# Attention and a two-layer MLP on one core: the Strassen product of the first layer from chunk 3 on instead of chunk 4

## The chip, the cores and the metric

The kernel runs on one core of a Trainium2 chip. A core has a matrix engine (TensorE, PE in the profile), a vector engine (VectorE, DVE), an engine for activations (ScalarE, ACT), a general one (GpSimd, POOL), a queue engine (SyncE, SP) and 16 DMA engines. They work side by side and wait for each other through semaphores. The metric is the device time of one launch in microseconds, as the median of several runs; less is better.

## The reference

Two parts follow each other. The first is attention with a sliding window of 128 positions and 4 sink positions, for 4 batches, 8 heads, 768 positions and 64 columns a head. The second takes the result as rows x of 512 columns:

```python
xn = (x - mu) / sqrt(var + 1e-6) * g_ln            # over the 512 columns
out = x + maximum(xn @ w_ch1, 0.0) @ w_ch2         # 512 -> 2048 -> 512
```

All inputs and the output are float32; the kernel works in bfloat16 with float32 sums.

## The kernel before

**Tiles and chunks.** The 3072 rows are 24 tiles of 128 rows. Two tiles are a chunk, so there are 12 chunks, three for each batch (R = 0, 1, 2 in the code). They are counted from 0 here, as in the code: the fourth chunk is chunk 3.

**What a chunk goes through.** Its q, k and v are loaded by DMAs on GpSimd's queue (lines 585 and 683). From chunk 4 on, q and k are turned by DMA transposes on SP's queue (line 685, which issues through the helper of line 565), once the scores of the chunk before are done. TensorE makes the scores in two halves (line 788), ScalarE the exponentials (line 802), VectorE multiplies by the mask (line 814). TensorE multiplies by v, one tile at a time (lines 833 and 838). VectorE then makes the rows: reciprocal, x, mean and variance (lines 852 to 860); GpSimd makes the root (lines 866 and 867); VectorE normalises (`xc`, line 869); from chunk 2 on SP turns the rows by DMA transposes (`xnt`, line 879, through the same helper). Then comes the MLP: the first layer into `hq`, the second into the output.

**Two forms of the first layer.** The plain form has eight groups `ph` of eight matmuls with 256 columns each (line 1011) and a relu for each (line 1021). From chunk `half` on, the first four of them are made by a Strassen product (Winograd's variant), `halves`, line 911: GpSimd makes four differences of `xnt` (line 922), TensorE seven products m1 to m7 of eight matmuls with 128 columns each (line 942), ScalarE copies three of them (`tz`, line 953), VectorE makes three totals (line 964), and ScalarE applies the relu to these (line 967) and to the fourth block (line 985). The products m5, m6, m7 and m3 use sums of the weights. These sums are made once, by four VectorE instructions (`weight_sums`, lines 897 to 909), into two buffers of the ring `hq`, which has eight; every chunk uses two.

**The second layer.** From chunk 2 on (`wino=2`) it is a Strassen product as well (`wino`, line 1058): sums of `hq` on VectorE (line 1076), seven products p1 to p7 on TensorE (line 1093), and additions on VectorE (lines 1107 and 1114).

**What sets the order.** No engine chooses anything at run time. The class `Plan` (line 65) simulates the kernel in the build: every operation has the engines that may take it, estimated times, the operations and buffers that it needs, and a due time (`prio`). In each step the planner takes the engine whose next operation can start first, and of those that can start within 0.25 units of that (0.2 on TensorE, 0 on SP) the one with the earliest due time. TensorE's operations with a due time of 40 or more go strictly by due time. The operations are issued in the order of their planned starts, so each engine's order is fixed. The planner's clock is an estimate; it runs some units behind the measured time.

**Due times that matter here.** With T = 16c + 8 for chunk c, the products of `halves` are due at T + `pos`, the four `ph` groups left at T + `pos4`, and the products of the second layer at T + 8.5 + 8/7 i. The attention of chunk c has its steps at

```python
def at(c, step):
    return 16.0 * c - 8.0 + (PAR["h"] if c > PAR["half"] else PAR)[step]
```

so `half` also divides the chunks into those whose attention goes by the numbers of `h` and those that go by the outer ones (`tr=-8.0, sc=-5.3, sc1=-2.0, av=2.0, avi=1.0`). In `h`, `tr` is for the transposes of q and k (the loads are due 14 before), `sc` and `sc1` for the two halves of the scores, `av` for the values, `avi` for the distance of the second tile, and `xo` for VectorE's row chain against `av`. Two more things hang on `c > half`: in chunks with R > 0 the mask of the first head pair (`mkp=(0,)`) is made by GpSimd in two instructions (line 809, due at `mko` behind the scores), not by VectorE. And from chunk `half` on, the planner reckons with a later landing of the transposed rows (`xlag`, line 880).

The other numbers: `wsum` is the due time of the first weight sum and the earliest planned start (the others 3 apart); `tlead` puts GpSimd's differences ahead, `tzp` the copies, `cpr` the totals; `sp` and `sq` place the sums of `hq` for the second layer, `kp` its additions.

Of the kernel before, what the change touches and what calls it, by code (L numbers as in the profile page):

```python
# [220 lines left out]
def fix(occ, extra=0.09):  # L221
# [17 lines left out]

PAR = dict(split=(3, 4, 5, 6, 7), gsum=-8.0, guard=183.0, strict=40.0, win=0.4, tr=-8.0, sc=-5.3, sc1=-2.0, av=2.0, trx=9.0, by_dma=4, x_by_dma=2, g_on_w=2, av2=20.0, avi=1.0, behind=5, gtt=9.0, ramp=0.3, vs0=2.6, vpb=12.0,  # L240
           w1p=(0.15, 1.7, 2.05, 2.8), pm=2, w2p=(4.5, 4.51, 4.52, 4.53), by_tile=2, wino=2, vp=(0.0, 0.1, 2.0, 2.1, 4.2, 4.3), ld1=0.05,
           h=dict(av=0.85, avi=-0.0, sc=-7.68, sc1=-2.94, tr=-24.25, trx=9.0, xo=-13.3), mkp=(0,), mko=-3.93, vsp=1, soon=0, lb=0, xlag=2.1, llag=2.4, mix=(1.0, 0.5), tzp=20.19, kp=-0.95, half=4, wsum=58.0, flip=1, te=("POOL",), tlead=58.56, rd=0, cpr=15.35, sp=(10.27, 4.87), sq=(-1.16, -17.0, 5.05, 17.16), pos=(-1.36, 0.58, 4.21, 6.8, 1.47, 1.55, 4.55), pos4=(4.77, 3.73, 4.73, 5.69))


def general(tc, nc, slots, pairs, ones, ident_f, ident, w1, w2, mhalf, g_s, g_r, q, k, v, out, scale):
# [1018 lines left out]
```

## Time and profile before

| | us |
|---|---|
| median of 3 runs | 209.54 |
| lowest and highest run | 208.6, 209.82 |
| the profiled execution's own time | 209.8 |
| its span, first to last instruction | 208.3 |
| PE busy in the span | 200.6 |
| DVE busy | 177.7 |
| ACT busy | 122.3 |
| POOL busy | 117.0 |

The span and the busy times are of one profiled execution. The busy time of TensorE is modelled from pipelined instructions. The mean granted clock of TensorE was 0.998 of full speed. A row of the profile names the line of the kernel, the engine, the operation, and the tiles written and read (`hq<-one`: from a PSUM bank `one` into `hq`). Operations that a helper issues carry the helper's line: all DMA transposes stand under line 565.

### The profile page before, as it was taken

The page shows a single profiled execution, that of the slowest core. Times are in us where ns is not written, and L with a number is a line of the kernel's source. Part 1 is how long each engine was busy: PE and PEld are TensorE (multiplying, and loading weights), DVE is VectorE, ACT ScalarE, POOL GpSimd, SP SyncE. Part 2 cuts the span into 40 slices and gives each one's busy share as a digit, 9 for nine tenths or more (in the row PEclk, how much of TensorE's full clock was granted, in tenths as well). Part 3 has the DMA queues.
Part 4 walks back from the last instruction along what each step waited for, and adds up shares of the span by engine and source line. Part 5 has one row for each costly group of instructions (what it writes and reads, how often), then busy time and mean ns, then how long its engine had stood idle before and what let it go on. Part 6 is the DMA issues. An engine that isn't in the chain of part 4 may idle for free.

```text
span 208.3 us, 6722 instructions
## 1 busy us (share of the span) xinstructions
PE 200.6 (96%) x2736; PEld 168.1 (81%) x2736; DVE 177.7 (85%) x433; ACT 122.3 (59%) x190; POOL 117.0 (56%) x170
## 2 busy tenths in 40 slices
PE   6978999999999999999999999999999999999994
PEld 2657897774698898997898997998988988998993
DVE  6579767999699898898879989989989979997783
ACT  3549379919455646466486586585586486471520
POOL 7965565369129119949639957888638038035000
PEclk9999999999999999999999999999999999999999
DMA  6999999999999999999999999999974511211202
GB/s 120 151 192 191 200 188 206 194 163 133 177 187 135 116 205 89 113 201 90 175 146 116 139 154 123 121 165 128 190 115 81 151 28 28 102 28 25 107 26 84
DMA packets 101245, 27.53 MB, mean 132 GB/s; under 512 B 89556, under 2 KB 99032, under 8 KB 101208
## 3 DMA queue, kind: packets, MB, share of 16 engines
q0 software_dynamic: 67712, 13.37, 77.8%
q1 hardware_dynamic: 33208, 13.41, 36.6%
q8 instruction: 22, 0.36, 0.7%
q10 hardware_dynamic: 288, 0.26, 0.4%
q14 instruction: 15, 0.12, 0.2%
HBM read 27.30 MB, written 6.29 MB: 161 GB/s over the span
## 4 chain that ended last, share of the span: by engine, by line
PE 85%; DMA 9%; POOL 3%; issue 1%; DVE 0%; SPq 0%
PE one L1093 28%; PE one L1011 20%; PE one L942 12%; PE one L1042 7%; DMA w<-in_moe_w_ch_dram 7%; PE one L1004 5%; PE pair L838 5%; PE pair L788 4%; DMA xnt<-xc 2%; PE pair L833 2%; PE one L668 1%; POOL nat L622 1%; POOL vn L585 1%; PE one L792 1%; POOL w L543 1%; POOL n4b L598 1%
## 5 line engine op out<-in xcount | busy, mean ns | idle before, releaser
L802 ACT ACTIVATE pe<-pair 128x1024 bf16<-128x1024 f32 (+1 forms) x40 | 36.3, 966 | 17.0 <-PE pair L788 17.0
L1011 PE MATMUL one<-xnt,w 128*128 128x256 bf16 x384 | 45.5, 273 | 0.0
L1021 ACT ACTIVATE hq<-one 128x512 bf16<-128x512 f32 x58 | 34.1, 594 | 19.4 <-PE one L1011 9.6
L1011 PEld LDWEIGHTS <-w 128*128 128x128 bf16 x384 | 36.6, 98 | 4.1
L1093 PEld LDWEIGHTS <-hs 128*128 128x128 bf16 x320 | 30.6, 98 | 3.9 <-DVE hs L1076 0.2
L866 POOL TENSOR_SCALAR st<-st 128x1 f32<-128x1 f32 x24 | 5.6, 235 | 44.3 <-DVE st L860 30.3
L967 ACT ACTIVATE hq<-hq 128x512 bf16<-128x512 bf16 x24 | 15.1, 628 | 19.7 <-DVE hq L964 19.7
L814 DVE TENSOR_TENSOR pe<-pe,mask 128x1024 bf16<-128x1024 bf16 (+1 forms) x35 | 25.5, 757 | 0.9 <-ACT pe L802 0.8
L1093 PEld LDWEIGHTS <-hq 128*128 128x128 bf16 x240 | 22.3, 98 | 4.1 <-issue 0.3
L585 POOL DMA_DIRECT2D vn<-in_v_dram x24 | 21.9, 920 | 3.2 <-DMA w<-in_moe_w_ch_dram 1.8
L953 ACT COPY tz<-one 128x512 f32<-128x512 f32 x24 | 13.3, 583 | 12.5 <-PE one L942 12.3
L1093 PE MATMUL one<-w,hq 128*128 128x256 bf16 x160 | 19.2, 273 | 0.0
L922 POOL TENSOR_TENSOR xt<-xnt 128x256 bf16<-128x256 bf16 x16 | 13.4, 855 | 8.9 <-DMA xnt<-xc 8.9
L1114 DVE TENSOR_TENSOR ot<-one,tm 128x256 f32<-128x256 f32 x40 | 16.2, 414 | 2.3 <-PE one L1093 1.9
L1107 DVE TENSOR_TENSOR tm<-one,x 128x256 f32<-128x256 f32 x40 | 16.7, 416 | 1.7 <-PE one L1093 1.5
L1076 DVE TENSOR_TENSOR hs<-hq 128x512 bf16<-128x512 bf16 x40 | 15.7, 421 | 2.5 <-ACT hq L1021 1.9
L1004 PE MATMUL one<-xnt,w 128*128 128x128 bf16 x256 | 16.3, 219 | 0.7 <-DVE xnt L891 0.5
L854 DVE TENSOR_TENSOR x<-pair,rec 128x512 bf16<-128x512 f32 x24 | 16.4, 691 | 0.7
L964 DVE TENSOR_TENSOR hq<-one,tz 128x512 bf16<-128x512 f32 x24 | 16.1, 674 | 0.7 <-PE one L942 0.4
L1004 PEld LDWEIGHTS <-w 128*128 128x128 bf16 x256 | 14.7, 98 | 2.0 <-issue 0.5
L683 POOL DMA_DIRECT2D nat<-in_k_dram x16 | 14.9, 930 | 2.5 <-DMA w<-in_moe_w_ch_dram 2.5
L683 POOL DMA_DIRECT2D nat<-in_q_dram x16 | 14.2, 898 | 3.6 <-DMA w<-in_moe_w_ch_dram 3.6
(131 smaller groups left out, 394.3 us busy)
## 6 DMA issues: line engine op xcount, KB each, us to landing
out_dram<-ot SPq DMA_DIRECT2D x17, 256.0 KB
w<-in_moe_w_ch_dram POOLq DMA_DIRECT2D x8, 512.0 KB, 13.1
vn<-in_v_dram POOLq DMA_DIRECT2D x24, 128.0 KB, 7.1
nat<-in_k_dram POOLq DMA_DIRECT2D x17, 128.0 KB, 4.8
nat<-in_q_dram POOLq DMA_DIRECT2D x17, 128.0 KB, 5.1
out_dram<-ot SPq DMA_DIRECT2D x14, 128.0 KB
kq<-nat SPq DMA_TRANSPOSE x32
xnt<-xc SPq DMA_TRANSPOSE x20
```

The source lines that it names most:

```text
L585: loads[b * RB + r, "v"] = P.op(f"vld{t}", {"POOL": (0.87, 0.9)}, prio, lambda e: G.dma_start(bv.t[:, :, 0:64], v[b, :, 128 * r:128 * (r + ...
L683: lambda e, nat=nat, ap=ap: G.dma_start(nat.t, ap), writes=[nat], dma=SW if c < 6 else (*SW[:2], PAR["llag"]), after=behind(c, 0 if soon e ...
L802: P.op(f"ex{c}{hp}", {"ACT": act(2 * n)}, d + 0.1 + 0.05 * j, lambda e, pp=pp, pb=pb: nc.scalar.activation(pb.t[:, :, 0:n], pp.t[:, :, 0:n ...
L814: V.tensor_mul(pb.t[:, :, 0:n], pb.t[:, :, 0:n], mm),
L854: P.op(f"x{t}", {"DVE": dve(512)}, d + xo + 0.11, lambda e: V.tensor_tensor(x.t.rearrange("p (a h c) -> p a h c", a=2, c=64), pv()[:, :, : ...
L942: nc.tensor.matmul(b.t[:, 128 * h:128 * h + 128], lhsT=lt[:, kk, 128 * h:128 * h + 128], rhs=rh[:, kk, :], start=first and h == 0 and kk = ...
L1004: nc.tensor.matmul(ph.t[:, 128 * s:128 * s + 128], lhsT=w1[u // 2][:, j, 128 * s:128 * s + 128], rhs=xnt.t[:, j, 128 * (u % 2):128 * (u % ...
L1011: nc.tensor.matmul(ph.t[:, 256 * s:256 * s + 256], lhsT=w1[ht // 4][:, j, 128 * (ht % 4):128 * (ht % 4 + 1)], rhs=xnt.t[:, j, :], start=j ...
L1021: nc.scalar.activation(hg.t[:, u % 4, :], ph.t, AF.Relu)
L1093: nc.tensor.matmul(at(r), lhsT=get(left, g)[:, v, s, :], rhs=rhs, start=first and n == 0, stop=n == 7, skip_group_check=True)
L1107: return P.op(f"tm{name}_{c}", {"DVE": dve(256, 1.14)}, pr - PAR["kp"], lambda e: V.tensor_tensor(tm[name].t, at(r), xs[i].t[:, sl], op=AL ...
L1114: return P.op(f"o{c}_{half}", {"DVE": dve(256, 1.14)}, pr - PAR["kp"], lambda e: V.tensor_tensor(ots[i].t[:, sl], at(r), tm[name].t, op=AL ...
```

## The change

One line of parameters is changed; no other code. In the diff below, the parameters that stay are left out:

```diff
@@ PAR (lines 240 to 242) @@
-           h=dict(av=0.85, avi=-0.0, sc=-7.68, sc1=-2.94, tr=-24.25, trx=9.0, xo=-13.3), mko=-3.93, tzp=20.19, kp=-0.95, half=4, wsum=58.0, tlead=58.56, cpr=15.35, sp=(10.27, 4.87), sq=(-1.16, -17.0, 5.05, 17.16), pos=(-1.36, 0.58, 4.21, 6.8, 1.47, 1.55, 4.55), pos4=(4.77, 3.73, 4.73, 5.69))
+           h=dict(av=0.83, avi=-0.0, sc=-7.76, sc1=-3.01, tr=-21.65, trx=9.0, xo=-13.67), mko=2.6, tzp=32.32, kp=-0.99, half=3, wsum=44.0, tlead=59.73, cpr=17.03, sp=(5.84, 8.08), sq=(-12.08, -25.59, 5.52, 11.11), pos=(-0.73, 0.43, 5.51, 8.02, 1.26, 3.01, 5.55), pos4=(7.47, 4.62, 5.73, 7.79))
```

With `half=3`, chunk 3 gets its first layer's half by `halves`: seven products instead of four `ph` groups, with the differences, copies, totals and relus that belong to them. `weight_sums` comes one chunk sooner, with a due time and an earliest start of 44, 47, 50 and 53 instead of 58, 61, 64 and 67. Chunk 4 is now behind `half`: its loads, transposes, scores and values go by `h`, and the mask of its first head pair goes from VectorE to GpSimd. The other numbers change the due times of the steps named above in all chunks that use them, so the planner may order them in another way.

More of the change, by code (lines that the diff above doesn't have):

```diff
@@ L241 @@
            w1p=(0.15, 1.7, 2.05, 2.8), pm=2, w2p=(4.5, 4.51, 4.52, 4.53), by_tile=2, wino=2, vp=(0.0, 0.1, 2.0, 2.1, 4.2, 4.3), ld1=0.05,
-           h=dict(av=0.85, avi=-0.0, sc=-7.68, sc1=-2.94, tr=-24.25, trx=9.0, xo=-13.3), mkp=(0,), mko=-3.93, vsp=1, soon=0, lb=0, xlag=2.1, llag=2.4, mix=(1.0, 0.5), tzp=20.19, kp=-0.95, half=4, wsum=58.0, flip=1, te=("POOL",), tlead=58.56, rd=0, cpr=15.35, sp=(10.27, 4.87), sq=(-1.16, -17.0, 5.05, 17.16), pos=(-1.36, 0.58, 4.21, 6.8, 1.47, 1.55, 4.55), pos4=(4.77, 3.73, 4.73, 5.69))
+           h=dict(av=0.83, avi=-0.0, sc=-7.76, sc1=-3.01, tr=-21.65, trx=9.0, xo=-13.67), mkp=(0,), mko=2.6, vsp=1, soon=0, lb=0, xlag=2.1, llag=2.4, mix=(1.0, 0.5), tzp=32.32, kp=-0.99, half=3, wsum=44.0, flip=1, te=("POOL",), tlead=59.73, rd=0, cpr=17.03, sp=(5.84, 8.08), sq=(-12.08, -25.59, 5.52, 11.11), pos=(-0.73, 0.43, 5.51, 8.02, 1.26, 3.01, 5.55), pos4=(7.47, 4.62, 5.73, 7.79))
 def general(tc, nc, slots, pairs, ones, ident_f, ident, w1, w2, mhalf, g_s, g_r, q, k, v, out, scale):
```

## The prediction

> **What bounds the kernel now.** I read the page first, for the busy shares and the chain that ended last; then TensorE's waits; then the chain in order of time around chunks 2 to 5; then the stretches between the first product of one chunk and of the next; then single engines. Chunks are counted from 0, so the fourth chunk is chunk 3. From the page:
>
> ```profile
> span 208.3 us, 6722 instructions
> PE 200.6 (96%) x2736; PEld 168.1 (81%) x2736; DVE 177.7 (85%) x433; ACT 122.3 (59%) x190; POOL 117.0 (56%) x170
> PE 85%; DMA 9%; POOL 3%; issue 1%; DVE 0%; SPq 0%
> ```
>
> TensorE (PE) is busy for 96% of the span and is 85% of the chain. The waits of PE, two rows of seven (released by, us in total, times, longest); the other five end by 23.05 us:
>
> ```profile
> PE one L1190 <- DVE ot L1114: 0.5, 1, 0.5
> PE one L942 <- DMA xnt<-xc: 0.4, 1, 0.4
> ```
>
> The chain in order of time (start, us, what):
>
> ```profile
> 23.05 1.07 PE one L1004 x16
> ...
> 58.52 4.37 PE one L1011 x40
> ...
> 64.64 0.46 PE pair L788 x22
> ...
> 68.51 1.85 PE one L1093 x16
> 70.36 1.75 PE one L1011 x16
> ...
> 88.54 0.89 PE one L942 x16
> ...
> 95.92 5.03 DMA xnt<-xc
> ...
> 101.00 0.61 PE one L942 x8
> ...
> 131.55 0.45 PE one L942 x8
> ...
> 146.79 0.45 PE one L942 x8
> ...
> 205.15 0.44 DVE ot L1114
> ```
>
> From 23.05 to 205.15 us the chain is PE instructions back to back with one break: PE waited 0.4 us at 101.00 for a DMA transpose of the normalised rows (xnt) of chunk 5. So in this stretch a microsecond of PE work is a microsecond of time, and idle time to be won is 0.4 us there and 0.5 us at the very end. Ahead of 23 us the planner places everything before any number of the change can act, so that part stays.
>
> **The change, part by part.** *PE work of chunk 3.* Four groups `ph` (u = 0 to 3), each 8 matmuls of 256 columns on line 1011, give way to seven products of 8 matmuls of 128 columns on line 942. Prices by the chain: 40 matmuls of line 1011 in 4.37 us, so 0.109 each; 16 of line 942 in 0.89 us, so 0.0556 each. Removed 32 x 0.109 = 3.50 us, added 56 x 0.0556 = 3.12 us: -0.38 us. Two whole stretches check it. The first begins with the last product of chunk 2 (70.36 - 0.87, half of the 16 matmuls at 68.51) and ends with the first product of chunk 4; the second is the same kind of stretch three chunks later, where the head of a batch is already done the new way (busy us of each engine behind the count):
>
> ```profile
> 69.49:85.36 15.87, 15.87 (x211) 13.76 (x210) 13.76 (x31) 9.66 (x14) 8.07 (x13) 1.00 1.41 139
> 115.99:131.55 15.56, 15.56 (x236) 13.78 (x233) 14.52 (x33) 10.15 (x16) 11.00 (x16) 1.00 1.42 143
> ```
>
> Both are PE-busy throughout, and the second is 0.31 us shorter. I take -0.35 us, between the two.
>
> The Trainium skill, page "TensorE: Matmul & The Clock Gate", section "Back-to-back issue gap", speaks against this: it gives about 81 ns per matmul as the sustained spacing at 128 columns, weight loads included. By that the 56 matmuls would take 4.54 us, the saving would be a loss of 1.04 us, and the sum would be 210.6 us. The trace does not agree: 16 such matmuls, each with a weight load of its own, took 0.89 us, or 56 ns each.
>
> *PE order.* By the numbers of the change (T = 16c + 8 for chunk c; products at T + pos, second-layer products at T + 8.5 + 8/7 i, scores at T - 23.76 and T - 19.01 and values at T - 15.17 of their chunk), the order from chunk 4 on is what it was: first product ahead of p3, second, both value tiles, m5, m6, one ph, m3, m7, three ph, m4, scores, p1 p2 p7 p6, scores, p4 p5. What moves is chunk 3's own stretch, which takes this order too, and the attention of chunk 4, which now counts as "behind half": its first scores go ahead of p1 of chunk 2, from 64.64 to 62.89 us (58.52 + 4.37, the end of chunk 2's first layer), and its second tile of values up to the first. These moves cost PE nothing if their inputs are there.
>
> *Are they there?* The DMA queue of SP, then VectorE's chain for tile 7, the last of chunk 3:
>
> ```profile
> 54.29 3.92 SPq L565 DMA_TRANSPOSE kq<-nat  x3
> 58.30 0.53 SPq L1054 DMA_DIRECT2D out_dram<-ot  x1
> 58.92 2.03 SPq L565 DMA_TRANSPOSE kq<-nat  x1
> ```
>
> ```profile
> 63.78 1.19 SPq L565 DMA_TRANSPOSE xnt<-xc  x1
> ```
>
> ```profile
> 57.20 0.21 DVE L852 RECIPROCAL rec<-pair 128x8 f32<-128x8 f32 x1 [1.23 <-PE pair L838]
> 62.19 0.68 DVE L907 TENSOR_TENSOR hq<-w 128x1024 bf16<-128x1024 bf16 x1
> 63.34 0.41 DVE L869 TENSOR_SCALAR xc<-x,st 128x512 bf16<-128x512 bf16 x1
> ```
>
> Chunk 4's four transposes of q and k must have landed by 62.89. The fourth starts at 58.92 behind a store; the longest landing that the chain shows is 5.03 us (95.92 to 100.95), in heavier traffic, which gives 63.95, or 1.06 us late. With the new due time (34.35 instead of 48) the four go ahead of that store (due 39.6), so the fourth starts near 58.2 and by the same landing is 0.35 us late; between 55 and 60 us no load was issued, so I take nothing and keep 0 to 1.06 for the range. The store then waits behind it; its buffer is one of four and is not asked for before chunk 3's sums.
>
> xnt of chunk 3: the second transpose starts at 63.78; with 5.03 us it lands at 68.81. The old order wanted it at 70.36, the new one at 69.49, since the first product goes ahead of p3. Slack shrinks from 1.55 to 0.68 us, still no wait. Value: nothing; bound: 0.5 us either way.
>
> *Weight sums.* Four VectorE instructions of 0.68 us, 2.7 us together, with planned earliest times 14 units sooner (the first ran at 62.19 for a planned 58, so now near 48 to 58). They must be ready for m5 of chunk 3, which stands three products and two value tiles behind 69.49, so past 72 us: 14 us spare. VectorE's cover is idle time such as the 1.23 us ahead of 57.20; the later places that they leave gain what the earlier lose. If that cover is gone a mask of chunk 3 is late by up to 0.68 us, and the values on PE behind it. Two more buffers of the `hq` ring are held for one chunk longer: 8 are there, chunks 1 to 3 and the sums use 8. Nothing.
>
> *Other engines in chunk 3.* Groups of the page (mean ns ahead of the last bar):
>
> ```profile
> L1021 ACT ACTIVATE hq<-one 128x512 bf16<-128x512 f32 x58 | 34.1, 594 | 19.4 <-PE one L1011 9.6
> L967 ACT ACTIVATE hq<-hq 128x512 bf16<-128x512 bf16 x24 | 15.1, 628 | 19.7 <-DVE hq L964 19.7
> L953 ACT COPY tz<-one 128x512 f32<-128x512 f32 x24 | 13.3, 583 | 12.5 <-PE one L942 12.3
> L964 DVE TENSOR_TENSOR hq<-one,tz 128x512 bf16<-128x512 f32 x24 | 16.1, 674 | 0.7 <-PE one L942 0.4
> L922 POOL TENSOR_TENSOR xt<-xnt 128x256 bf16<-128x256 bf16 x16 | 13.4, 855 | 8.9 <-DMA xnt<-xc 8.9
> ```
>
> ScalarE loses 4 x 0.594 and gains 3 x 0.583 + 3 x 0.628 + 0.6 = +1.9 us on 9.66 of 15.87: room. VectorE gains 3 x 0.674 = 2.0, loses the fourth weight sum (0.68) and one mask of chunk 4 that goes out of the stretch with the scores (0.64, half of the row below): 13.76 to about 14.5 of 15.5. GpSimd (POOL) gains four sums at some 0.8 us and, ahead of the stretch, the first mask of chunk 4. The stretch 115.99 to 131.55 carries all that (VectorE 14.52, ScalarE 10.15, POOL 11.00) without one idle PE slot.
>
> ```profile
> 70.20 1.28 DVE L814 TENSOR_TENSOR pe<-pe,mask 128x1024 bf16<-128x1024 bf16 x2
> ```
>
> So: nothing, as long as the order is no worse than there. Chunk 4's six loads get an earlier due time too; each waited for an older weight load, not for its turn,
>
> ```profile
> 33.59 0.87 POOL L683 DMA_DIRECT2D nat<-in_k_dram x1 [0.85 <-DMA w<-in_moe_w_ch_dram]
> ```
>
> so they do not move, and what is queued behind them does not either.
>
> *The sum.* -0.35 us, and no wait added or removed. The profiled execution took 209.8 us (span 208.3 and 1.5 around it), so 209.45 on its own terms; it lies 0.26 above the median of 209.54, so the forecast is 209.54 - 0.35 = **209.2 us**.
>
> **The rivals.** *Slower: xnt late in every chunk.* The first product of each chunk waits for both transposes, and the trace shows how thin this is. POOL's first sum starts as xnt lands:
>
> ```profile
> 114.99 1.74 POOL L922 TENSOR_TENSOR xt<-xnt 128x256 bf16<-128x256 bf16 x2 [0.39 <-DMA xnt<-xc]
> 131.13 2.24 POOL L922 TENSOR_TENSOR xt<-xnt 128x256 bf16<-128x256 bf16 x2 [2.01 <-DMA xnt<-xc]
> 146.49 1.83 POOL L922 TENSOR_TENSOR xt<-xnt 128x256 bf16<-128x256 bf16 x2 [1.24 <-DMA xnt<-xc]
> ```
>
> PE wants it at 115.99, 131.55 and 146.79: slack 1.0, 0.4 and 0.3 us, and -0.4 at 101.00; chunk 3 joins with 0.68. If VectorE's new order makes the rows late by 1 us, the waits are 0.3 + 1.0 + 0 + 0.6 + 0.7 = 2.6 us, less 0.35: 211.8 us. It decides from about 0.5 us of lateness on. What could make it late:
>
> ```profile
> 80.76 1.26 POOL L809 TENSOR_SCALAR_AFFINE_SELECT pe<-pe 128x512 bf16<-128x512 bf16 x2
> ```
>
> ```profile
> 80.81 1.50 DVE L1076 TENSOR_TENSOR hs<-hq,hs 128x512 bf16<-128x512 bf16 x1
> ```
>
> ```profile
> L1076 DVE TENSOR_TENSOR hs<-hq 128x512 bf16<-128x512 bf16 x40 | 15.7, 421 | 2.5 <-ACT hq L1021 1.9
> ```
>
> A VectorE sum that takes 0.42 in the mean took 1.50 beside POOL's mask, +1.1 us, and the change brings such a mask to chunk 4 and four POOL sums to chunk 3. The Trainium skill, page "SBUF — State Buffer", section "SBUF: two separate sides", says why: VectorE with two SBUF inputs and GpSimd share a port pair under an exclusive lock; these two rows agree. Against the rival: VectorE's due times for the row chain move only from 12.35 to 12.74 ahead of the T of the chunk before, still behind two of its totals and ahead of the third. Chance 0.24, with lateness of chunk 4's transposes in it.
>
> *A little faster: the wait at 101.00 goes as well.* -0.35 - 0.4 gives 208.8 us. For it: chunk 4's second value tile comes earlier, so VectorE is freer ahead of chunk 5; against: chunk 5's own rows are ordered as before. Chance 0.17.
>
> *Faster still.* All idle time that PE has behind 23 us (0.4 + 0.5) and 0.35: 208.3 us; or part of it and a lucky draw of the runs, which lay 1.2 us apart before. Chance 0.11.
>
> *The products run no faster than their weight loads.* The page has them at 98 ns:
>
> ```profile
> L1011 PEld LDWEIGHTS <-w 128*128 128x128 bf16 x384 | 36.6, 98 | 4.1
> ```
>
> One behind the other, 56 of them take 5.5 us, +2.0, 211.2 us with nothing else. The 0.0556 above speaks against it. Chance 0.01, put with slower.
>
> **How the numbers follow.** The forecast has 0.47, the little gain 0.17, faster still 0.11, slower 0.25. A measurement of this kernel can tell about 0.5% (1.05 us) from no change. Forecast and little gain lie inside it, but for a small part; of the slower case 0.03 stays inside. So faster 0.11, same 0.67, slower 0.22. Range: down to 208.3, all idle gone; up to 211.2, which takes in the 1.06 us of the transposes and half of the slower rival. The likeliest case's own range is 208.7 to 209.9.
>
> **What would show it.** Line 1011 has 352 matmuls instead of 384 and line 942 56 more; the first product of chunk 3 starts near 69.5 us and that of chunk 4 near 85.0, without a gap. The weight sums lie between 47 and 58 us. Wrong are my steps if PE waits for `kq` at 62.9 (transposes), for `xnt` at 69.5 or more than 0.4 us in all later (rival), or for VectorE's `hq`, `hs` or `pe` in chunks 2 to 4.

## The result and the profile after

| | before | after |
|---|---|---|
| median, us (6 runs each, on one chip) | 209.37 | 212.39 |
| lowest to highest, us | 208.59 to 210.5 | 211.21 to 212.85 |
| the profiled execution, us | 209.8 | 212.47 |
| its span, us | 208.3 | 210.9 |

After against before is 1.0129, with a 95% interval of [1.0095, 1.0162]: the change makes the kernel 3 us slower. The forecast was 209.2 us with a range up to 211.2, so it was wrong, and in its sign too. The page of the kernel after:

```profile
span 210.9 us, 6772 instructions
PE 200.9 (95%) x2755; PEld 168.4 (80%) x2760; DVE 182.8 (87%) x435; ACT 122.5 (58%) x193; POOL 123.0 (58%) x176
q14 instruction: 17, 0.13, 0.3%
PE 53%; DMA 3%; DVE 3%; SPq 0%; issue 0%
L1011 PE MATMUL one<-xnt,w 128*128 128x256 bf16 x352 | 41.9, 273 | 0.0
```

TensorE is busy for as long as before (200.9 against 200.6 us), but the span is 2.6 us longer. VectorE has 5 us more of busy time with only two instructions more in that count. Line 1011 has the 352 matmuls foreseen. The shares of the chain add up to 59% only, since it can't be followed back further than 82.77 us.

**First part: the end.** Where does the span end, counted from the last instruction of TensorE (line 1190)? That one starts at 205.63 us before and at 206.65 after; the span ends 2.67 us later before and 4.23 us later after. So 1.56 us of the loss stand behind all the work. The view of line 1224, the branch at the end (duration min/median/max in ns, first and last start in us), shows it. VectorE (DVEq) and ScalarE (ACTq) before:

```profile
L1224 ACTq COMPARE_BRANCH  x1: 50/50/50, 199.6 to 199.6; - x1
L1224 ACTq EVENT_SEMAPHORE  x1: 17/17/17, 202.3 to 202.3; - x1
L1224 DVEq COMPARE_BRANCH  x1: 72/72/72, 205.8 to 205.8; - x1
L1224 DVEq EVENT_SEMAPHORE  x1: 21/21/21, 206.4 to 206.4; - x1
```

The same two rows of VectorE after:

```profile
L1224 DVEq COMPARE_BRANCH  x1: 72/72/72, 206.8 to 206.8; - x1
L1224 DVEq EVENT_SEMAPHORE  x1: 21/21/21, 209.8 to 209.8; - x1
```

The closing handshake after (line 1259): one of SyncE's semaphore waits takes 1718 ns, where before the longest of the fourteen was 28.

```profile
L1259 SPq EVENT_SEMAPHORE  x14: 17/28/1718, 207.5 to 210.8; - x14
```

Between the branch and the next instruction of VectorE lie 0.60 us before and 2.97 after (the unrounded starts), and everybody waits for VectorE. This is called the gap below. The fallback's code, `general`, lies behind this branch, and a good input jumps over it. ScalarE pays such a gap in the kernel before as well, 199.6 to 202.3, but six microseconds ahead of the end, where nobody waits. GpSimd has one too (193.72 to 196.44). The trace has 520 entries on VectorE before and 524 after.

What happens in the gap? The queue that brings instructions (q14) shows it. Its row for the packets that start from 208.0 to 209.7 us after:

```profile
q14 instruction: 1, 0.01, 1.4%
```

That packet, 8 KB, starts at 208.29, 1.49 us behind the branch, and VectorE goes on 1.48 us later. Before, no packet of q14 starts between VectorE's branch and its next instruction.

**Second part: waits of TensorE.** The view of waits, after (released by, us in total, times, longest):

```profile
PE one L1093 <- DVE ot L1114: 1.1, 1, 1.1
PE pair L788 <- DMA kq<-nat: 0.6, 2, 0.4
PE one L1190 <- DVE ot L1114: 0.5, 1, 0.5
```

The last was there before. The first two are new: 1.7 us, in place of the 0.4 us for `xnt` at 101.00, which is gone. In the timeline of TensorE after (start, duration, idle time ahead in brackets):

```profile
62.20 0.33 PE L788 MATMUL pair<-kq 64*64 64x192 bf16 x8 [0.43 <-DMA kq<-nat]
...
86.10 1.03 PE L1093 MATMUL one<-w,hs 128*128 128x256 bf16 x8 [1.15 <-DVE ot L1114]
```

The first is the transposes of chunk 4, at the place that the prediction named. The second is a product of chunk 3's second layer, whose PSUM bank (`one`, the tile that the product writes) VectorE has to read first. VectorE's timeline at that place, then GpSimd's:

```profile
83.02 2.68 DVE L1076 TENSOR_TENSOR hs<-hq,hs 128x512 bf16<-128x512 bf16 x2
85.63 0.41 DVE L1114 TENSOR_TENSOR ot<-one,tm 128x256 f32<-128x256 f32 x1
85.97 2.28 DVE L814 TENSOR_TENSOR pe<-pe,mask 128x1024 bf16<-128x1024 bf16 x2
```

```profile
83.48 1.31 POOL L922 TENSOR_TENSOR xt<-xnt 128x256 bf16<-128x256 bf16 x2
84.74 1.49 POOL L922 TENSOR_TENSOR xt<-xnt,xt 128x256 bf16<-128x256 bf16 x2
```

Two sums that take about 0.4 us each took 2.68 us while GpSimd made its differences, and the `ot` behind them was late. The chain that ended last goes through VectorE here, from 82.77 to 88.26 us: the sums and `ot`, and then the two masks, which hold up the values of line 838 at 88.30.

The two parts together: TensorE's last instruction came 1.02 us later though the head was 1.3 us faster in this execution (the first matmul of line 1011 at 53.7 against 55.0; the wait for the first load, line 668, is 0.5 against 1.4 us; over the runs it reaches 1.8, and two executions don't list it). So the stretch between them is 2.3 us longer, and the end 1.56. The listed waits make up 1.34 of the 2.3 (1.74 against 0.40). They count from the modelled end of the matmul ahead, so they leave part out: the product at 86.10 starts 1.76 us behind the one ahead of it, the same product of chunk 2 starts 0.45 behind (69.12 and 68.67), so this place cost 1.31 us and not 1.15.

### The profile page after: what moved, and what is told of

Read it like the earlier page. It is cut to its first block, busy times and chain, and to the rows that moved or that the text cites. A ratio compares the mean times of both kernels' runs of the same rounds, so it can differ in the third digit from the quotient of the medians.

```text
span 210.9 us, 6772 instructions
## 1 busy us (share of the span) xinstructions
PE 200.9 (95%) x2755; PEld 168.4 (80%) x2760; DVE 182.8 (87%) x435; ACT 122.5 (58%) x193; POOL 123.0 (58%) x176
## 4 chain that ended last, share of the span: by engine, by line
PE 53%; DMA 3%; DVE 3%; SPq 0%; issue 0%
PE one L1093 24%; PE one L1011 12%; PE one L942 11%; DMA kq<-nat 3%; PE pair L838 3%; PE pair L788 3%; DVE hs L1076 1%; DVE pe L814 1%; PE pair L833 1%; PE one L792 0%; DVE ot L1114 0%; SPq L565 0%; DVE tm L1107 0%; PE one L1190 0%; PE one L1184 0%
## 5 line engine op out<-in xcount | busy, mean ns | idle before, releaser
L1011 PE MATMUL one<-xnt,w 128*128 128x256 bf16 x352 | 41.9, 273 | 0.0
L1021 ACT ACTIVATE hq<-one 128x512 bf16<-128x512 f32 x54 | 31.4, 595 | 14.0 <-PE one L1004 8.5
L1011 PEld LDWEIGHTS <-w 128*128 128x128 bf16 x352 | 33.5, 98 | 3.8
L967 ACT ACTIVATE hq<-hq 128x512 bf16<-128x512 bf16 x27 | 16.9, 628 | 28.2 <-DVE hq L964 28.2
L814 DVE TENSOR_TENSOR pe<-pe,mask 128x1024 bf16<-128x1024 bf16 (+1 forms) x34 | 29.6, 901 | 0.3 <-ACT pe L802 0.3
L1093 PEld LDWEIGHTS <-hq 128*128 128x128 bf16 x240 | 22.1, 98 | 4.2 <-issue 0.3
L953 ACT COPY tz<-one 128x512 f32<-128x512 f32 x27 | 14.9, 583 | 12.3 <-PE one L942 12.3
L964 DVE TENSOR_TENSOR hq<-one,tz 128x512 bf16<-128x512 f32 x27 | 18.1, 672 | 0.1
L942 PEld LDWEIGHTS <-hq 128*128 128x128 bf16 x288 | 17.2, 98 | 0.6
L858 DVE BATCH_NORM_STATS2 st<-x 128x6 f32<-128x512 bf16 x24 | 15.9, 686 | 0.2
```

The costliest lines, as they stand in the source:

```text
L814: V.tensor_mul(pb.t[:, :, 0:n], pb.t[:, :, 0:n], mm),
L942: nc.tensor.matmul(b.t[:, 128 * h:128 * h + 128], lhsT=lt[:, kk, 128 * h:128 * h + 128], rhs=rh[:, kk, :], start=first and h == 0 and kk = ...
L964: o = P.op(f"c{n}_{c}", {"DVE": dve(512, 1.14)}, pr, lambda e: V.tensor_tensor(block(n), banks_[bank].t.rearrange("p (i t) -> p i t", i=4) ...
L967: P.op(f"r{n}_{c}", {"ACT": act(512), "DVE": dve(512, 0.26)} if PAR["rd"] else {"ACT": act(512)}, pr + 0.1, lambda e: nc.scalar.activation ...
L1011: nc.tensor.matmul(ph.t[:, 256 * s:256 * s + 256], lhsT=w1[ht // 4][:, j, 128 * (ht % 4):128 * (ht % 4 + 1)], rhs=xnt.t[:, j, :], start=j ...
L1021: nc.scalar.activation(hg.t[:, u % 4, :], ph.t, AF.Relu)
```

## The experiments

Two explanations were set against each other first: the end (VectorE's program became a few instructions longer, and its last branch then lacks its target), called theory A, and what happens in the chunks. For the latter, theory B says that VectorE and GpSimd hold each other up in chunk 3's new Strassen product; its rival is the new order alone. Later theories are named where they come. All ratios are to the kernel before, run beside it on the same chip. The diffs leave out the parameters that stay.

**b_pad.** Before, with one constant written five times; four more instructions on VectorE early on, nothing else.

```diff
-    constant("ones_f", "DVE", 0.06, 7.0, lambda e: V.memset(ones_f, 1.0), writes=[Bc["ones_f"]])
+    constant("ones_f", "DVE", 0.06, 7.0, lambda e: [V.memset(ones_f, 1.0) for _ in range(5)], writes=[Bc["ones_f"]])
```

> The kernel before with one change: the memset of ones_f on VectorE is issued five times instead of once, so VectorE's program is four instructions longer, as many as it executes more in the changed kernel (524 against 520), and nothing else moves. In the profiles VectorE's first instruction behind the last branch comes 2.97 us after it in the changed kernel and 0.60 us in the one before. Theory A (where the branch's target lies in VectorE's program decides whether its instructions are there in time): the tail from the last TensorE instruction to the end of the span grows from 2.7 to about 4.2 us, time 209.4 + 1.6 = 211.0 us. Rival (the long tail of the changed kernel comes from its last stores or is chance): tail 2.7 us, time 209.4 to 209.6 us.

211.51 us, 1.008 [1.0042, 1.0119]. The view of line 1224:

```profile
L1224 DVEq COMPARE_BRANCH  x1: 72/72/72, 204.7 to 204.7; - x1
L1224 DVEq EVENT_SEMAPHORE  x1: 21/21/21, 207.9 to 207.9; - x1
```

524 entries, 3.2 us behind the branch, span ending 4.48 us behind the last TensorE instruction; TensorE's waits in the chunks are 0.25 us. Four tiny instructions with no part in the work cost 1.6 us of the median (1.8 us at the end of the profiled execution).

**a_hint.** After, with the branch hint given for VectorE too.

```diff
-    tc.mark_branch_hint_location("all_is_well", engines=[mybir.EngineType.PE])
+    tc.mark_branch_hint_location("all_is_well", engines=[mybir.EngineType.PE, mybir.EngineType.DVE])
```

> The changed kernel with one change: the branch hint that TensorE has for the last branch is given to VectorE too (one more VectorE instruction). Theory A: VectorE's wait behind the branch goes, tail about 2.7 instead of 4.25 us, time 212.4 - 1.6 = 210.8 us; the TensorE part stays as it is, with its wait of about 1.1 us before the last product of chunk 3's second layer. Rival (stores or chance): 212.4 us.

210.29 us, 1.0018 [0.9975, 1.006]. The gap is back at 0.62 us, the end at 2.67. The wait of about 1.1 us that was expected to stay is not there, neither in this execution nor in the two later ones of the same program; this one waits 0.39 us for `xnt` and 0.50 for `hs` instead. The view of line 1224, then that of line 1259 with the hint at the start of VectorE's program:

```profile
L1224 DVEq COMPARE_BRANCH  x1: 84/84/84, 207.3 to 207.3; - x1
L1224 DVEq EVENT_SEMAPHORE  x1: 21/21/21, 207.9 to 207.9; - x1
```

```profile
L1259 DVEq BRANCH_PREFETCH_HINT  x1: 51/51/51, 1.0 to 1.0; - x1
```

With b_pad this shows both directions: a longer program of VectorE makes the gap, the hint takes it away. The packet of q14 agrees in every trace. In the five executions with the gap on VectorE (after, after2, b_pad, b_half3, a_sq) one starts 1.48 to 1.62 us behind its branch; in the twelve without it none starts between that branch and VectorE's next instruction. (The packet 0.5 to 0.6 us behind TensorE's branch is in all seventeen.) Only the place tells; the totals of q14 on the pages do not: a_hint2 has 16 without the gap and after2 has 16 with it.

The Trainium skill, page "Runtime: NRT & Kernel Launch", section "Instruction fetch mechanics", says that a taken branch whose target lies outside the two pages of instructions that an engine holds must fetch it by DMA before it goes on. The gap of 2.97 us against 0.60 and the packet inside it agree; where the boundary lies no run shows beyond 520 entries without the gap and 524 with it on VectorE. It is not the count alone that decides: ScalarE has the gap with 252 entries. GpSimd shows the same in the other direction in a_te_hint below: 215 entries in place of 263, 0.47 us behind its branch in place of 2.82 in a_hint, and no packet there.

**b_half3.** Before, with the Strassen half from chunk 3 and the earlier weight sums, and the old other numbers.

```diff
-           half=4, wsum=58.0
+           half=3, wsum=44.0
```

> The kernel before with half=3 and wsum=44 alone, every other number as before: the Strassen product in chunk 3 without the other order. Theory B (TensorE's loss of about 2 us between 61 and 89 us comes from the new Strassen chunk: VectorE's sums for the last product of chunk 3 are held up beside GpSimd's differences, and chunk 4's transposes are late): a wait of 0.5 to 1.5 us at the last products of chunk 3's second layer here too, last TensorE instruction at least 0.5 us later than in the kernel before, as far as the starts of the two executions agree. Rival (the other order alone does it): no such wait, the TensorE part 0.35 us shorter than before. By theory A the tail is long if VectorE executes 524 instructions.

212.33 us, 1.0091 [1.0044, 1.0137]; 525 entries, gap 3.04, end 4.31 us. The half alone already lengthens VectorE's program over the point. The wait that theory B foresaw at the last products of chunk 3's second layer did not come; TensorE waited for `xnt` (0.29 and 0.58 us) and for two masks (0.25 and 0.24).

**a_sq.** After, with the old places of the sums for the second layer.

```diff
-           sp=(5.84, 8.08), sq=(-12.08, -25.59, 5.52, 11.11)
+           sp=(10.27, 4.87), sq=(-1.16, -17.0, 5.05, 17.16)
```

> The changed kernel with sp and sq of the kernel before, so that VectorE's sums for the second layer have their old due times. Rival to theory B (the new due times put the last sums, s4, right in front of the last product): the wait of 1.15 us before the last product of chunk 3 goes, time 212.4 - 1.2 = 211.2 us. Theory B: the sums are late because VectorE is slowed beside GpSimd, whichever of its own instructions comes first; the wait stays within 0.5 us of 1.15 or moves to the next consumer, time 212 to 212.6 us.

211.48 us, 1.0048 [1.001, 1.0085], end 4.39 us. In its profiled execution, which at 210.19 us lies 1.3 below the median, only the `kq` wait is left in the chunks (0.42 us). VectorE, then GpSimd, at the place of the 1.15 us:

```profile
82.69 0.75 DVE L1076 TENSOR_TENSOR hs<-hq,hs 128x512 bf16<-128x512 bf16 x2
```

```profile
83.15 1.44 POOL L922 TENSOR_TENSOR xt<-xnt 128x256 bf16<-128x256 bf16 x2
84.56 2.19 POOL L922 TENSOR_TENSOR xt<-xnt,xt 128x256 bf16<-128x256 bf16 x2
```

GpSimd starts 0.46 us behind VectorE in both kernels (83.48 - 83.02, 83.15 - 82.69). Here VectorE's two sums take 0.75 us and GpSimd's four 3.6; in the kernel after 2.68 and 2.8. So one of the two loses, and the order in the code doesn't say which.

**b_hint, b_half3_hint, a_half4_hint, a_hint2.** All with the hint of a_hint, so that the end is the same and the rest can be read: the kernel before; before with `half=3, wsum=44.0`; after with `half=4, wsum=58.0`, which is the new order without the half; and a_hint again.

```diff
# b_half3_hint, beside the hint
-           half=4, wsum=58.0
+           half=3, wsum=44.0
# a_half4_hint, beside the hint
-           half=3, wsum=44.0
+           half=4, wsum=58.0
```

> The kernel before with the branch hint for VectorE as well. Theory A: its VectorE already goes on 0.60 us behind the last branch, so nothing is won: time within 0.3% of before, tail 2.7 us. It is the base of the three kernels beside it, all with this hint, so that the tail is the same in all four. Rival (the hint shortens the time by something else than the wait behind the branch): over 0.5 us faster than before.

> The kernel before with half=3 and wsum=44 and the hint: the Strassen product in chunk 3 alone, without the long tail. Theory B (VectorE and GpSimd hold each other up in the new Strassen chunk): 0 to +1 us against before, since the loss eats the 0.35 us of TensorE work. Rival (the prediction's sum, -0.35 us): 209.0 to 209.5 us when before is 209.6.

> The changed kernel with half=4 and wsum=58 and the hint: the other order alone. Theory B: within 0.3% of before, since the order of the later chunks is nearly the same. Rival (the other order makes the rows late in every chunk): over 1 us slower than before, with waits of TensorE for xnt or kq in several chunks.

> The changed kernel with the hint once more, on the same chip as the three beside it: the whole change without the long tail. Theories A and B: 0 to +1 us against before (it was 0.18% slower, with an interval from -0.25% to 0.6%), so the tail is the greater part of the 1.3%. Rival (half or more of the loss sits in the TensorE part): 1 to 1.5 us slower than before.

| | us | ratio | end, us |
|---|---|---|---|
| b_hint | 209.89 | 1.0011 [0.9979, 1.0044] | 2.71 |
| b_half3_hint | 210.17 | 1.0012 [0.9984, 1.0039] | 2.71 |
| a_half4_hint | 210.64 | 1.0036 [1.0002, 1.007] | 2.67 |
| a_hint2 | 210.6 | 1.0036 [1.001, 1.0061] | 2.67 |

The hint does nothing for the kernel before, which has no gap to lose. The half without its end costs nothing that can be measured, and gains nothing either. The other numbers, without the half, cost 0.36%, and TensorE waits for `xnt` (0.51 and 0.45 us) and `ot` (0.57) there. With the half on top (a_hint2) it is 0.36% as well.

**a_c4_hint and b_half3_c4_hint.** Theory C: the waits come because chunk 4, now behind `half`, has its attention by `h`. So `c > PAR["half"]` becomes `c > 4` in all four places (lines 551, 805, 824, 851), in a_hint and in b_half3_hint.

```diff
-        return 16.0 * c - 8.0 + (PAR["h"] if c > PAR["half"] else PAR)[step]
+        return 16.0 * c - 8.0 + (PAR["h"] if c > 4 else PAR)[step]
...
-                if R and c > PAR["half"] and hp in PAR["mkp"]:
+                if R and c > 4 and hp in PAR["mkp"]:
```

> The changed kernel with the hint, and chunk 4's attention counted as ahead of half again (c > 4 in place of c > half in its four places): its scores, values and first mask stand where the kernel before has them; chunk 3 keeps its Strassen product. Theory C (what is left of the loss without the tail, 0.36%, is chunk 4's attention pulled ahead of its transposes and GpSimd's extra mask): no wait for kq near 62 us, time 0.4 to 0.8 us below the changed kernel with the hint, so 209.6 to 210.1 us when before is 209.8. Rival (the Strassen chunk itself costs it on VectorE and GpSimd): no gain, 210.4 to 210.8 us.

> The kernel before with half=3, wsum=44, the hint, and chunk 4's attention kept as before: the Strassen product in chunk 3 with everything else as it was. The prediction's sum for this alone is -0.35 us: 209.2 to 209.7 us when before is 209.8, and it would be the best of all. Theory C: this gain shows, 0.1 to 0.3% faster than before. Rival (the chunk is paid back on VectorE beside GpSimd): 209.8 to 210.4 us.

210.69 us, 1.0065 [1.0036, 1.0094], and 211.9 us, 1.009 [1.0053, 1.0128]; the end is 2.67 us in the second. The wait for `kq` goes, as it must, but nothing is won: others come. The waits of b_half3_c4_hint:

```profile
PE one L942 <- DMA xnt<-xc: 2.7, 3, 1.3
```

Theory C falls: chunk 4's early attention is not what costs. With it put back in b_half3_c4_hint, TensorE waits for the rows of chunks 3 to 5, and the time is above that of b_half3_hint (1.0012) by more than the intervals.

**a_te_hint.** Theory D: GpSimd's differences slow VectorE's sums and masks. In a_hint, VectorE makes the differences itself.

```diff
-           te=("POOL",)
+           te=("DVE",)
```

> The changed kernel with the hint, and the four differences of xnt in each Strassen chunk on VectorE instead of GpSimd (36 instructions of about 0.2 us more on VectorE, 36 of about 0.8 us less on GpSimd). Theory D (VectorE's sums and masks of two SBUF operands stand still while GpSimd works on SBUF): the mean of the masks of line 814 and of the sums of line 1076 falls towards 0.68 and 0.42 us, VectorE's busy time grows by less than the 7 us that the new instructions take, and TensorE no longer waits before the last product of the second layer. Rival (VectorE is slow there by its own queue): masks and sums keep their means, busy time grows by 7 us or more, and the time grows by 1 us or more.

223.49 us, 1.069 [1.0635, 1.0745]. The durations go as theory D has it. Groups by form (busy us, mean ns of one ahead of the last bar), after and then a_te_hint:

```profile
L814 DVE TENSOR_TENSOR pe<-pe,mask 128x1024 bf16<-128x1024 bf16 x22 | 21.7, 1013 | 0.3 <-ACT pe L802 0.3
L1076 DVE TENSOR_TENSOR hs<-hq,hs 128x512 bf16<-128x512 bf16 x20 | 11.1, 584 | 0.0
```

```profile
L814 DVE TENSOR_TENSOR pe<-pe,mask 128x1024 bf16<-128x1024 bf16 x22 | 18.2, 855 | 0.1
L1076 DVE TENSOR_TENSOR hs<-hq,hs 128x512 bf16<-128x512 bf16 x20 | 8.4, 420 | 0.0
L922 DVE TENSOR_TENSOR xt<-xnt 128x256 bf16<-128x256 bf16 x18 | 4.4, 284 | 4.9 <-DMA xnt<-xc 4.9
```

VectorE took over 9.6 us of work (36 differences, two forms) and its busy time grew from 182.8 to 186.2 only; a mask takes 0.16 us less. But the differences now stand in VectorE's own order, which waits 4.9 us for `xnt` there, and TensorE waits for the sums behind:

```profile
PE one L1093 <- DVE hs L1076: 7.7, 8, 2.6
```

That is a kernel with another bound, so it prices the contention but does not say what the contention costs the kernel after.

**after2, a_hint3, a_sp_hint, b_sp_hint.** Theory E: of the other numbers, the exchange of the two halves in `sp` makes the sums collide. The kernel after and a_hint again, a_hint with the halves exchanged back, and b_hint with them exchanged.

```diff
# a_sp_hint, beside the hint
-           sp=(5.84, 8.08)
+           sp=(8.08, 5.84)
# b_sp_hint, beside the hint
-           sp=(10.27, 4.87)
+           sp=(4.87, 10.27)
```

> The changed kernel as it is, on the same chip as the three beside it. Theory A: 1.6 us above the same kernel with the hint, so about 1.2% slower than before; tail 4.2 us again, VectorE's first instruction behind the branch about 3 us after it. Rival (the first measurement was high by chance): within 0.5 us of the kernel with the hint.

> The changed kernel with the hint, third time, as the base on this chip: 0.2 to 0.5% slower than before by theories A and E; tail 2.7 us.

> The changed kernel with the hint and the two numbers of sp exchanged, (8.08, 5.84): VectorE makes the sums of the first half of the blocks ahead of those of the second, as the kernel before does and as the products read them. Theory E (what is left without the tail is this exchange: p6 and p3 read the first half first, and it came second): TensorE's waits for hs at p6 (0.2 to 0.3 us, in chunks 3 and 6) and before p3 go, time 0.5 to 1 us below the kernel with the hint beside it, so 0.3% faster to 0.1% slower than before. Rival (the rest is noise or the Strassen chunk): no difference to the kernel with the hint.

> The kernel before with the hint and the two numbers of sp exchanged the other way, (4.87, 10.27): the second half's sums first, half=4 and all else as before. Theory E: waits of TensorE for hs at line 1093 appear that the kernel before does not have, in sum 0.5 us or more, and the time is 0.2 to 0.6% above before. Rival: within 0.2% of before, no such waits.

| | us | ratio | end, us | waits of TensorE in the chunks, us |
|---|---|---|---|---|
| after2 | 211.79 | 1.009 [1.0054, 1.0126] | 4.26 | 0.35 kq, 1.13 ot, 0.29 hs |
| a_hint3 | 211.05 | 1.0044 [1.0007, 1.008] | 2.66 | 0.17 + 0.21 kq, 0.90 xnt, 0.18 + 0.31 hs |
| a_sp_hint | 210.32 | 1.0001 [0.9965, 1.0038] | 2.66 | 0.41 xnt |
| b_sp_hint | 209.83 | 0.9982 [0.9948, 1.0016] | 2.66 | none |

Exchanged back, the waits for `hs` go; exchanged in the kernel before, they don't come. So theory E as it stood falls: the exchange alone costs nothing, at most together with the rest of the new order, and even there the intervals of a_hint3 and a_sp_hint overlap. Chunk 6 shows how near it is. VectorE, GpSimd and TensorE of a_hint3:

```profile
127.71 1.60 DVE L1076 TENSOR_TENSOR hs<-hs,hq 128x512 bf16<-128x512 bf16 x1
```

```profile
127.77 1.25 POOL L809 TENSOR_SCALAR_AFFINE_SELECT pe<-pe 128x512 bf16<-128x512 bf16 x2
```

```profile
129.37 1.05 PE L1093 MATMUL one<-n4c,hs 128*128 128x256 bf16 x8 [0.31 <-DVE hs L1076]
```

VectorE and GpSimd of a_sp_hint at the same place:

```profile
127.78 0.53 DVE L1076 TENSOR_TENSOR hs<-hs,hq 128x512 bf16<-128x512 bf16 x1
```

```profile
127.97 1.88 POOL L809 TENSOR_SCALAR_AFFINE_SELECT pe<-pe 128x512 bf16<-128x512 bf16 x2
```

GpSimd starts 0.06 us behind VectorE in the one and 0.19 in the other; the sum takes 1.60 or 0.53 us, GpSimd's pair 1.25 or 1.88.

## Why the prediction was wrong, point by point

**The step that failed: "-0.35 us, and no wait added or removed", with "span 208.3 and 1.5 around it" left as it was.** What lies behind the last instruction of TensorE was carried over as fixed. It is not: the half adds instructions on VectorE (b_half3 has 525 entries against 520), and with them its last branch pays for its target. The price could have been read from the trace of before: ScalarE's 199.6 to 202.3 is that gap on an engine without the hint. Whether the change would bring VectorE to it could not. The prediction counted VectorE's new work in microseconds (2.0 more, 1.3 less) and never asked what a few instructions more do to the program's length.

How much it is, in three ways that agree: the end in the profiled executions, 4.23 and 4.26 against 2.67, +1.6 us; b_pad alone, +0.8%, 1.6 us; and the kernel after with and without the hint, the mean of 1.0129 and 1.009 against the mean of 1.0018, 1.0036 and 1.0044, 0.8%, 1.6 us. That is the larger part of the loss, and it is shown.

**The rest, about 0.3% or 0.7 us.** Waits of TensorE in the chunks, summed over each profiled execution: in the changed order 1.74 (after), 1.77 (after2), 0.89, 2.33 and 1.77 (the three with the hint), 1.7 in the mean; in the old order 0.40 (before), 0.25 (b_pad), 1.13 (b_hint) and 0 (b_sp_hint), 0.45 in the mean. So the change adds about 1.25 us of listed waits, and less PE work gives 0.2 to 0.35 of it back. That is the size of the rest, within the intervals, but it is argued and not shown. From the first matmul of line 1011 to line 1190 the same five executions took 2.0 us more than the four in the mean, and they lie 0.8 us above the medians of their kernels, the four 0.1 below. And the half alone has waits of the same size: 1.36 us in b_half3, and 1.87 in b_half3_hint, whose median shows no loss. The places move from one execution to the next too: the 1.15 us for `ot` at 86.10 came in both executions of the kernel after and in none of the three with the hint. Which of the new numbers brings the waits is not settled: a_half4_hint has them without the half (1.0036), and no single number that was put back decided it beyond the intervals.

*PE work of chunk 3, "I take -0.35 us".* Sign right, size a little less. From the first product of chunk 3 to that of chunk 4, in the stretches of the kernel after, TensorE was busy without a gap:

```profile
68.67:84.34 15.67, 15.67 (x235) 13.84 (x232) 14.66 (x31) 9.82 (x17) 11.28 (x17) 1.00 1.27 144
```

15.67 us against 15.87 is -0.20, with VectorE at 14.66 and GpSimd at 11.28, as foreseen from the later stretch (14.52 and 11.00). So the analog held where it was taken from, inside chunk 3. In the end b_half3_hint shows no gain: 1.0012 [0.9984, 1.0039], where -0.35 us alone would be 0.9983; its profiled execution waited 1.2 us for one chunk's `kq`. The rule of 81 ns that would have made +1.04 us of it is not seen here either: the eight products from 68.67 on took 0.45 us, 56 ns each.

*"Are they there?"* Taken at nothing for `kq`, with 0.35 us by the longest landing and 1.06 as the bound. SyncE after:

```profile
53.00 5.39 SPq L565 DMA_TRANSPOSE kq<-nat  x4
58.49 1.15 SPq L1054 DMA_DIRECT2D out_dram<-ot  x1
```

The four go ahead of the store, as foreseen, and TensorE still waits, 0.43, 0.42, 0.35, 0.63 and 0.17 us in five of the executions (after, a_sq, after2, a_hint2, a_hint3). The middle value of 0.35 was the right one to take; "no load was issued" was no reason for nothing. The longest landing, 5.03 us, was one row of one execution: on the chains of the other executions the transposes took 3.93 to 7.01 us, at this very place 5.16 (a_sq) and 5.44 (a_hint2), and in the old order 6.15 (b_hint) and 6.79 (b_pad). For `xnt` of chunk 3 the slack of 0.68 us held in after, and did not in a_hint (0.39), a_hint3 (0.90), a_c4_hint (0.73), a_sp_hint (0.41) and b_half3 (0.58): the bound of 0.5 was too narrow.

*Weight sums.* Right: they ran at 52.38, 53.10, 55.31 and 55.91 us, 0.68 each, and nobody waited.

*"Nothing, as long as the order is no worse than there".* The condition was the weak place. The stretch taken as proof has the same work without a wait, but in one execution and one order. The wait of 1.15 us at 86.10 is just what the rows of the lock (1.50 for 0.42) had warned of, one chunk later, where GpSimd's differences for chunk 4 meet VectorE's sums of chunk 3. The Trainium skill, page "SBUF — State Buffer", section "SBUF: two separate sides", has VectorE and GpSimd share a port pair under an exclusive lock; the pairs above (2.68 and 2.8 us, or 0.75 and 3.6) agree in so far as one of the two is held up each time. Which one is not to be read from the starts: VectorE starts first in all four pairs shown above and is held up in two.

*The rivals.* "xnt late in every chunk" gave 211.8 us, near the result, by a cause that did not act: the profile after has no wait for `xnt` in the chunks. The little gains (208.8 and 208.3) asked for the wait at 101.00 to go; it went in the kernel after, and larger ones came. The price of the weight loads was added up wrongly: +2.0 us on 209.54 is 211.5 and not 211.2; it didn't act either. No rival had the end of the program, so the chance of slower, 0.22, was too small for a reason whose price was in the trace.

No version was shown to be faster than the kernel before; b_sp_hint, the lowest, is 0.9982 [0.9948, 1.0016].

## What to carry to other kernels

Look behind the last working instruction as well: where a branch stands there, count what a change adds to the program of each engine that ends late, and give the branch hint to all of these, since an engine that pays the fetch early may hide it. When a change promises 0.2%, the tenths of a microsecond that decide transfers and the lock between VectorE and GpSimd are larger than the gain; a stretch elsewhere that carries the same load without a wait does not show that they fall the same way again. Take the middle of a lateness that the rows bound, not nothing, where the slack is smaller than the spread of the landings, and take that spread from more than one execution.

## What was not expected of the hardware

- Four instructions more on an engine, 520 to 524, cost 1.6 to 1.8 us at a taken branch at the very end, though b_pad's stand ahead of all chunks, far from that branch; with the hint the gap is 0.62 us. An instruction packet starts inside each such gap, on ScalarE and GpSimd too.
- The contention of VectorE and GpSimd is two-sided, and a few tenths decide who pays: a VectorE sum 0.53 or 1.60 us, GpSimd's pair of masks 1.88 or 1.25.
- Taking 9.6 us of small sums over from GpSimd raised VectorE's busy time by only 3.4 us (182.8 to 186.2), because its other instructions got shorter.
- The start varies by more than the change was forecast to be worth: the first matmul of line 1011 at 54.43, 54.69 and 55.34 us in three executions of one program (a_hint), with the wait for the first load 0.46, 1.83 and 1.48.
